# Second sine table from the first's angle, k's first block loaded ahead of x's second quarter, two ScalarE copies ahead of the fold, and the order anew

## The chip, the cores and the metric

The kernel runs on one core of a Trainium2 chip. A core has five engines with queues of their own: TensorE (PE, matrix products into PSUM; its weight loads are listed as PEld), VectorE (DVE, element-wise work), ScalarE (ACT, functions from tables, and copies), GpSimd (POOL) and SyncE (SP, which here only issues DMAs). Each engine works through its instructions in the order in which the program issues them and waits on semaphores where another engine or a transfer has to be done first. The metric is device time in microseconds (us); lower is better.

## The reference

Two parts, whose results stand side by side in the last dimension. A is dilated sliding attention over x with 32 heads of 18, a window of 8 and a dilation of 2. B is a causal long convolution with a short one ahead of it, all per channel.

```python
# S = 2048, D = 576, H = 32, Dh = 18, W = 8, dil = 2, ks = 4
def A(x, wqkv, wo):
    q, k, v = split(x @ wqkv)                       # each (H, S, Dh)
    idx = pos[:, None] - arange(W)[None, :] * dil    # 8 positions back, every second
    logits = einsum("hsd,hswd->hsw", q, k[:, idx]) * Dh ** -0.5    # idx < 0 masked
    return einsum("hsw,hswd->hsd", softmax(logits), v[:, idx]) @ wo

def B(q, k, v, shift_k, ssm_k, ssm_D):
    k_shift = sum(k shifted by t positions * shift_k[:, t] for t in range(4))
    kv = k_shift * v
    y = irfft(rfft(kv, 2 * S) * rfft(ssm_k, 2 * S))[:S]     # causal convolution over S
    return q * (y + kv * ssm_D)
```

## The kernel before, in words

All inputs are bf16. Part A is computed with the sequence along the free dimension: x is transposed (its first two quarters of 512 positions by TensorE, `transpose_x`, L477 to L481; the other two by transposing DMAs, `turn_x`), and `project` (L386) makes q, k and v tile by tile: eight matmuls of 128x512 and two for the last 64 rows, then one ScalarE copy out of PSUM (L427). `project_first` (L507) makes q's tiles for the first half of the sequence earlier. The logits are VectorE products of q with shifted k (L849) that TensorE sums over each head's rows (L864); softmax, the weighing of v (L973 with sums at L990) and the output product (L1046) follow.

Part B splits the sequence into four blocks of 512 and does the convolution as products of short spectra. For each block i, `taps(i)` (L582) is VectorE's work: k shifted and weighted by the taps `skb` and multiplied by v. `mirror(i, n)` (L610) folds the block's two halves with TensorE and copies the result back with ScalarE (L620). `x_spectrum(i)` (units "fx", L793 and L795) and `filter_spectrum(m)` (units "fk", L638, L639 and L714) are matmuls with sine tables. `fold_filter(m)` (L668) prepares the filter's block m first: for m = 0 to 2 by four ScalarE copies (L674 to L677) and three indirect DMAs of POOL's queue that gather and add rows (`gather`, L652); for m = 3 by matmuls (`by_matmuls`, L683), with the copies of L691 and L692 and then two copies out of PSUM (L694). A block's spectra are multiplied on VectorE (L1126), summed over blocks on TensorE (L1154) and turned back (`inverse`, L1186), and the result is gated with q.

**Sine tables.** Each matmul table holds sines at integer phases. `table` (L449) forms the phases with two VectorE multiplications (L451) and one bitwise and (L452), and returns a ScalarE call that takes the sine of 128x1024 phases (L453). Before the change there are two tables for the filter (`table_k(0)`, `table_k(1)`) and two for x (`table_x(0)`, `table_x(1)`), a quarter period apart, and each has its own phases. The four calls stand in the list `sines` and are issued between the first projections (L554, L557, L569).

**Loads.** Nearly all loads go through SP's queue, in program order: x's first quarter, w's first part, x's second quarter (`load_x(1)`), k's first block (`load_k(0)`, six DMAs on SP and a small one on POOL's queue, and a POOL memset of three rows that lie before the sequence), w's second part, v's first block, k's second, and so on.

**The order.** Up to the projections the order is written out by hand. From there, pieces of TensorE work with their ScalarE copy ("units") lie in one list, `units`. VectorE's work is emitted in a fixed order, and at set places `until()` (L361) takes the next number out of PLACES and pops so many units from the head of the list; `need(label)` (L368) pops until no unit with that label is left. So the number tuples at the top of the file settle how the work of TensorE and ScalarE falls between VectorE's steps. Each tile of projections is two units, of which the first has 0 and the second 1 as its third argument; the code uses this to insert nothing between them. What the tuples do:

- PLACES: the first four numbers are popped after `taps(0)` to `taps(3)`, the fifth before the logits, the next five within the first half's logits (then the second half's logits, softmax and the rest).
- AT: where the mirrors of blocks 0 to 2 and fold 3 are inserted into the list.
- EARLY: how many units of filter spectrum 3 stand before, between and after the two mirrors of block 3.
- FKS and FXS: how units of the x spectra and of v's projection are mixed with those of the filter spectra 3, 2, 1, 0.
- FOLDS: where folds 2, 1 and 0 are inserted, in this order of insertion, at most at the first unit that needs them.
- REGROUP: before which steps of the logits VectorE regroups v's weights.
- ZMIX, BY_DMA, PRE: when, in the loop over n = 1 to 26 at L1315, spectral products begin, and which sums of spectra go by DMA (`third`, L1067: an SP copy and an adding DMA of POOL's queue). A number above 26 in BY_DMA or PRE is never reached.

PSUM is two pools, tags A and B, of two buffers each: a unit's matmuls wait until an earlier unit's ScalarE copy has freed a buffer.

Of the kernel before, what the change touches and what calls it, by code (L numbers as in the profile page):

```python
# [16 lines left out]
PSUM = bass.MemoryType.PSUM  # L17

ZMIX = (
    3, 1, 0, 0, 1, 5,  # L20
)

PRE = (
    27, 33,
)

TOGETHER = (
# [3 lines left out]
THIRDS = ((0, 0), (0, 1), (1, 1)), ((0, 2), (1, 2)), ((0, 3), (1, 3))  # L31

BY_DMA = (
    37, 32, 21,
)

REGROUP = (
    0, 7,
)
# [6 lines left out]
FKS = (  # L46
    5, 1, 0, 0, 0, 0, 0, 0, 0, 0, 0, 0, 0, 0, 0, 0, 0, 0, 0, 2, 0, 0, 0, 0, 0, 1, 0, 0, 2, 0,
)
FXS = (
    0, 1, 1, 25, 2, 0, 0, 0, 0,  # L50
)

FOLDS = (
    2, 5, 9,
)

EARLY = (
    0, 0, 6,
)

AT = (
    0, 8, 9,
)


# [6 lines left out]
def kernel(  # L72
# [13 lines left out]
    nc = tc.nc  # L86
# [92 lines left out]
    nc.scalar.dma_start(skrow[96:97, :], B_shift_k.rearrange("d j -> (d j)").unsqueeze(0))  # L179
    warm = sp1.tile([128, 1], FP32, name="warm")  # L180
    nc.scalar.activation(warm[:], pib[:], ACT.Sin)
# [29 lines left out]
    def load_k(i):  # L211

        eng = nc.sync
        kj = sp1.tile([128, 7, D], BF16, name="kj", bufs=2)
        r0 = BL * i
        low = [(0, 64)]
        if i == 0:
            nc.gpsimd.memset(kj[0:1, 0:3, :], 0.0)
            nc.gpsimd.dma_start(kj[0:1, 3:7, :], kf[0:4, :].unsqueeze(0))
            low = [(1, 49), (49, 64)]  # L220
        for a, b in ((3, 7), (0, 3)) if i == 0 else ((0, 7),):
            for p0, p1 in low:
                eng.dma_start(kj[2 * p0:2 * p1:2, a:b], bass.AP(
                    tensor=kf.tensor, offset=kf.offset + (r0 + 4 * p0 - 3 + a) * D,
                    ap=[[4 * D, p1 - p0], [D, b - a], [1, D]]))
            eng.dma_start(kj[1:128:2, a:b], bass.AP(tensor=kf.tensor, offset=kf.offset + (r0 + 256 + 3 - a) * D,
                                                    ap=[[4 * D, 64], [-D, b - a], [1, D]]))
        kjs.append(kj)
# [217 lines left out]
    nc.vector.tensor_copy(rp[:], rp_i[:])  # L446
    nc.vector.tensor_scalar(rp[64:128, 4:8], rp[64:128, 4:8], -510.0, None, op0=ALU.add)

    def table(n_i, T, vec, cols, period, offs):  # L449
        for n in range(2):  # L450
            nc.vector.tensor_scalar(n_i[:, n, :], vec, rp[:, cols[n]:cols[n] + 1], offs[n], op0=ALU.mult, op1=ALU.add)  # L451
        nc.vector.tensor_single_scalar(n_i, n_i, period - 1, ALU.bitwise_and)  # L452
        return lambda: nc.scalar.activation(T, n_i, ACT.Sin, bias=pib[:], scale=-2.0 * np.pi / period)  # L453

    def table_k(c):
        return table(n_all[:, 2 * c:2 * c + 2, :], TK[:, c, :, :], n_all[:, 8, :], (2 + c, 2 + c), 2048, (256.0, 1792.0))

    def table_x(n):
        return table(n_all[:, 4 + 2 * n:6 + 2 * n, :], TX[:, 2 * n:2 * n + 2, :], n_all[:, 8, :], (4, 5), 4096,
              (512.0 + 1024.0 * n,) * 2)  # L460

    def table_i(s):

# [204 lines left out]
    def fold_filter(m):  # L668
# [14 lines left out]
        def by_matmuls():  # L683
            pss = [bank2("ps_rev", "A") for _ in range(2)]
            for c in range(2):
                turns = ((flip0, 1 - c), (corner, c), ((identn0, identn)[c], 2 + c))
                for n, (w, of) in enumerate(turns):
                    for h in range(2):
                        nc.tensor.matmul(pss[c][:, h, 0:HD], w[:], kt[:, of, HD * h:HD * h + HD], start=(n == 0),
                                         stop=(n == len(turns) - 1))  # L690
            nc.scalar.activation(other(m), kt[:, 2, :], ACT.Copy, scale=keep2[:])  # L691
            nc.scalar.activation(row(m, 2), row(m, 2), ACT.Copy, scale=0.5 / KAPPA)  # L692
            for c in range(2):
                nc.scalar.activation(halves(kt[:, c, :]), pss[c][:, :, 0:HD], ACT.Copy, scale=0.5)  # L694
                pe(0.7, "A", 0.65)
            nc.gpsimd.dma_start(view(Ks, k_at(m, 2) + 2 * D, [[1, 2 * D]]), view(Ks, k_at(m, 2), [[1, 2 * D]]),
                                accum_op=ALU.add, max_dma_last_dim=2 * D)
            nc.gpsimd.dma_start(other(m), kt[:, 0, :], accum_op=ALU.add)

        if m == NBL - 1:  # L700
            return (1.4, by_matmuls, f"fold{m}")
        return (0.0, unit, f"fold{m}")

    def filter_spectrum(m):
# [27 lines left out]
    def add_half(t, to, of):  # L732
        nc.gpsimd.dma_start(half(t, to), half(t, of), accum_op=ALU.add, max_dma_last_dim=HB)

    def turn_filter(m):
        for part in range(2):
            add_half(Ks, k_at(m, part), k_at(m - 1, part))
# [3 lines left out]
    for i in range(NBL):  # L741
# [634 lines left out]
```

## Time and profile before

| what | value |
|---|---|
| median of 3 runs | 214.44 us (214.31 to 215.56) |
| the profiled execution | 215.43 us |
| its span in the profile | 213.7 us |
| instructions | 5043 |
| matmuls on TensorE | 2094 |
| DMA traffic | 40.84 MB, 191 GB/s on average |

The page's slices show how evenly the engines are busy; each digit is the busy share of a fortieth of the span (5.3 us) in tenths:

```profile
PE   7899899999597989998999999999999999999891
...
DVE  7999999999989948969888999989969999899952
ACT  4699788765989989988358878864865887765540
POOL 8999990001958888422175000002029002313000
PEclk9999999999969999999999999999999999999998
DMA  6999999998153587999999999494779977995133
```

A 9 is 90% or more. PEclk is the clock granted to TensorE in tenths of full speed. A row of the timeline gives the start in us, the duration in us, the engine, the line of the kernel, the operation, what is written and read with its shape, how many instructions the row merges, and in brackets the idle time of the engine just before it with what ended that idle time. An engine name with a small q stands for its sequencer, where DMAs are issued; SPq is the loads' queue. The DMA table's last column is the time from issue to landing. Where a wait names an engine that had long been done, the real releaser was another one, often a DMA.

### The profile page before, as it was taken

Reading aid. Unit: us, or ns where it says so; the run is one execution under the profiler, and the core shown is the slowest. Engines: PE = TensorE matmul, PEld = TensorE weight load, DVE = VectorE, ACT = ScalarE, POOL = GpSimd, SP = SyncE. Lnnn points to the kernel's source line nnn. Section 1 sums busy time; section 2 is a strip of 40 time slices with the busy share of each in tenths; the row PEclk is TensorE's granted clock in tenths of the full one; section 3 lists DMA queues with packets and bytes.
Section 4 is the critical chain, followed back from the end, with each engine's and each line's share of the span. In section 5 each row is a group of like instructions: output and inputs, shape, how many; then the busy total and the mean of one; then the engine's idle time right before and its main releaser. Section 6 shows DMA issues by size and latency. Waiting matters only on the chain.

```text
span 213.7 us, 5043 instructions
## 1 busy us (share of the span) xinstructions
PE 199.4 (93%) x2094; PEld 109.7 (51%) x2094; DVE 191.5 (90%) x143; ACT 156.1 (73%) x226; POOL 83.6 (39%) x106
## 2 busy tenths in 40 slices
PE   7899899999597989998999999999999999999891
PEld 3443444344342455465334666666566667676660
DVE  7999999999989948969888999989969999899952
ACT  4699788765989989988358878864865887765540
POOL 8999990001958888422175000002029002313000
PEclk9999999999969999999999999999999999999998
DMA  6999999998153587999999999494779977995133
GB/s 203 294 323 235 240 326 330 217 239 227 59 83 55 86 114 104 181 188 150 220 237 238 207 217 215 72 225 140 155 276 195 205 224 254 215 236 198 38 110 110
DMA packets 35866, 40.84 MB, mean 191 GB/s; under 512 B 17442, under 2 KB 28834, under 8 KB 35844
## 3 DMA queue, kind: packets, MB, share of 16 engines
q1 hardware_dynamic: 27490, 25.76, 46.5%
q0 software_dynamic: 5888, 12.25, 31.6%
q10 hardware_dynamic: 2466, 2.51, 3.5%
q8 instruction: 16, 0.26, 0.5%
q14 instruction: 6, 0.05, 0.1%
HBM read 15.32 MB, written 5.61 MB: 98 GB/s over the span
## 4 chain that ended last, share of the span: by engine, by line
PE 34%; issue 8%; DMA 7%; DVE 4%; ACT 4%; POOL 2%; ACTq 0%; DVEq 0%; POOLq 0%
PE ps_z L1154 9%; PE ps_inv L1186 7%; PE ps_wo L1046 6%; PE ps_acc L990 6%; DMA Ks<-Ks 4%; PE ps_fx L793 3%; DMA qk<-in_A_wo_dram 3%; DVE av L973 2%; ACT av L1167 2%; PE ps_wo L1038 1%; DVE qk L973 1%; POOL qk L1022 1%; ACT qk L994 1%; DVE TB L1195 1%; PE ps_back L1227 1%
## 5 line engine op out<-in xcount | busy, mean ns | idle before, releaser
L391 PE MATMUL ps_proj<-xw 128*128 128x512 bf16 x160 | 38.1, 380 | 0.5 <-ACT qk L427 0.5
L849 DVE TENSOR_TENSOR av<-qk 128x4096 bf16<-128x4096 bf16 (+1 forms) x16 | 31.7, 2020 | 4.5 <-PE ps_log L864 3.9
L391 PEld LDWEIGHTS <-xw 128*128 128x128 bf16 x160 | 14.2, 98 | 20.2 <-issue 5.9
L1126 DVE TENSOR_TENSOR qk<-xw,Ks 128x2304 bf16<-128x2304 bf16 x16 | 21.0, 1349 | 0.0
L427 ACT ACTIVATE qk<-ps_proj 128x1024 bf16<-128x1024 f32 x14 | 14.3, 1025 | 8.7 <-PE ps_proj L402 4.1
L1167 ACT ACTIVATE av<-ps_z 128x768 bf16<-128x768 f32 x20 | 15.3, 809 | 6.7 <-PE ps_z L1154 6.7
L714 ACT ACTIVATE Ks<-ps_fk 128x576 bf16<-128x576 f32 x32 | 18.7, 666 | 1.6 <-PE ps_fk L639 1.6
L588 DVE TENSOR_TENSOR tB<-kj,skb 128x4608 bf16<-128x4608 bf16 (+1 forms) x8 | 19.3, 2418 | 0.1
L795 ACT ACTIVATE xw<-ps_fx 128x576 bf16<-128x576 f32 x32 | 18.5, 662 | 0.8 <-PE ps_fx L793 0.8
L793 PE MATMUL ps_fx<-xw,TB 128*128 128x288 bf16 x128 | 17.9, 286 | 1.1 <-ACT v L427 0.5
L652 POOL DMA_INDIRECT Ks<-bounce,from_row x8 | 16.4, 2053 | 5.1 <-ACT Ks L676 3.0
L1046 PE MATMUL ps_wo<-qk 128*128 128x288 bf16 x128 | 17.9, 287 | 0.0
L638 PE MATMUL ps_fk<-Ks,TB 128*128 128x384 bf16 x62 | 17.5, 339 | 0.1
L1073 POOL DMA_DIRECT2D xw<-xw x3 | 3.6, 1204 | 32.4 <-DMA xw<-xw 30.9
L990 PE MATMUL ps_acc<-av,ident 64*64 64x512 bf16 x160 | 15.7, 378 | 0.2 <-DVE av L973 0.2
L639 PE MATMUL ps_fk<-Ks,TB 128*128 128x192 bf16 x62 | 15.7, 253 | 0.0
L793 PEld LDWEIGHTS <-TB 128*128 128x128 bf16 x128 | 11.9, 98 | 7.2 <-issue 4.2
L973 DVE TENSOR_TENSOR av<-Ks,v 128x4096 bf16<-128x4096 bf16 x6 | 13.7, 2289 | 2.0 <-PE ps_acc L990 1.1
L1046 PEld LDWEIGHTS <-qk 128*128 128x128 bf16 x128 | 11.5, 98 | 5.9 <-issue 3.4
L1189 ACT ACTIVATE v<-ps_inv 128x576 bf16<-128x576 f32 (+1 forms) x14 | 9.5, 675 | 6.9 <-PE ps_inv L1186 6.9
L994 ACT ACTIVATE qk<-ps_acc 128x1024 bf16<-128x1024 f32 x8 | 8.2, 1024 | 8.1 <-PE ps_acc L990 8.1
L1186 PE MATMUL ps_inv<-av,TI 128*128 128x288 bf16 (+1 forms) x96 | 13.4, 293 | 0.6 <-ACT av L1167 0.6
(196 smaller groups left out, 458.0 us busy)
## 6 DMA issues: line engine op xcount, KB each, us to landing
Ks<-Ks POOLq DMA_DIRECT2D x8, 576.0 KB, 6.7
TB<-av SPq DMA_DIRECT2D x12, 256.0 KB, 6.1
kj<-in_B_k_dram SPq DMA_DIRECT2D x6, 504.0 KB, 5.7
vt<-in_B_v_dram SPq DMA_DIRECT2D x8, 288.0 KB, 5.0
Ks<-av SPq DMA_DIRECT2D x8, 256.0 KB, 6.7
xw<-xw SPq DMA_DIRECT2D x3, 576.0 KB
xw<-xw POOLq DMA_DIRECT2D x3, 576.0 KB, 8.7
Ks<-in_A_x_dram SPq DMA_DIRECT2D x2, 576.0 KB, 4.1
```

Of the source, the lines that this page charges most:

```text
L391: nc.tensor.matmul(ps[:, jp, :], wq(kb, comp, 128 * ct, 128), xT(kb, 1024 * jj + 512 * jp, 512), **se)
L588: dve(2304 * n, lambda: nc.vector.tensor_tensor(to, view(kj, row * D, [[D, n], [D, 4], [1, D]]), view(skb, row * D, [[D, n], [0, 4], [1, D ...
L714: nc.scalar.activation(view(Ks, k_at(m, cs ^ (m & 1)) + 96 * gi, [[768, 3], [384, 2], [1, 96]]), acc3(ps), ACT.Copy, scale=(PSG, MSG)[cs][ ...
L793: nc.tensor.matmul(ps[:, pm, 0:HD], TX[:, 2 * pm + c, 128 * gi:128 * gi + 128], kv[:, 2 * c + pm, HD * h:HD * h + HD], start=(c == 0), sto ...
L849: return P, at, step, dve(1024 * nj, lambda: nc.vector.tensor_tensor(view(P, at, [[step, 4], [256, nj], [1, 256]]), view(t, o + 256 * hh, ...
L973: r = dve(4096, lambda: nc.vector.tensor_tensor(view(P, 0, [[2048, 2], [256, W], [1, 256]]), X, view(v, voff + 2 + 256 * hh, [[512, 2], [2 ...
L990: nc.tensor.matmul(acc[64 * o:64 * o + 64, h, :], ident[64 * h:64 * h + 64, 64 * h:64 * h + 64], view(P, 256 * u, [[2048, 2], [1, 256]])[6 ...
L1046: nc.tensor.matmul(ps[:, r, 0:HD], oT(hh, 2 * c + r, t)[:, o:o + 128], wo[:, t // 2, t % 2, HD * h:HD * h + HD], start=(t == 0 and h == 0) ...
L1126: r = dve(3 * QTR, lambda: nc.vector.tensor_tensor(pr, view(xw, HB * XG[i] + QTR * t, [[HB, 3], [1, QTR]]), view(Ks, k_at(j - i, 0) + QTR ...
L1154: nc.tensor.matmul(view(acc[r], 512 * h, [[192, 2], [96, 2], [1, 96]])[o:o + 64], w[64 * h:64 * h + 64, 64 * h:64 * h + 64], pr[64 * h:64 ...
L1167: nc.scalar.activation(y, z, ACT.Copy)
L1186: nc.tensor.matmul(ps[:, c, 0:n], TI[:, sl, pm, 128 * c:128 * c + 128], Y(j, pm)[:, sl, c0:c0 + n], start=(pm == 0 and sl == 0), stop=(sl ...
```

## The change

Four edits and a new set of order numbers.

1. `table` now makes both tables of a pair from one set of phases: VectorE forms the phases once, ScalarE takes the sine (first table), then the absolute value of the same angle into fp32, and later the sine of a quarter turn minus or plus that absolute value (second table). Two [128, 1] constants for the quarter turns are set by POOL.
2. `load_k(0)` moves ahead of `load_x(1)`. The three rows before the sequence are filled by a DMA on ScalarE's queue from a zeroed row, in place of the POOL memset.
3. The two ScalarE copies of fold 3 that need no matmul (L691, L692) become `kept`, which is issued with the first half of the next projection tile that starts behind the list's second unit.
4. Numbers in ZMIX, PRE, BY_DMA, REGROUP, PLACES, FKS, FXS, FOLDS, EARLY and AT.

```diff
-    3, 1, 0, 0, 1, 5,
+    3, 1, 0, 0, 0, 2,
 PRE:       -27, 33,      +30, 32,
 BY_DMA:    -37, 32, 21,  +38, 30, 24,
 REGROUP:   -0, 7,        +2, 15,
 PLACES = (
-    6, 11, 13, 5, 1, 1, 3, 4, 11, 3, 9, 3, 3, 1, 2, 5, 3, 4, 0, 5, 0, 5, 5, 6, 2, 5, 4, 1, 2, 1, 2, 12, 2, 2, 3,
-    1, 0, 5, 1, 2, 0, 3, 1, 9, 12, 1, 1, 0, 2, 11, 0, 0,
+    3, 14, 13, 6, 1, 3, 3, 2, 10, 4, 11, 0, 4, 0, 3, 5, 3, 4, 1, 4, 0, 5, 5, 5, 3, 5, 4, 1, 2, 1, 2, 12, 2, 2, 3,
+    1, 0, 5, 1, 2, 4, 4, 0, 5, 6, 1, 1, 0, 11, 0, 8, 2,
 FKS (30 numbers):  second 1 -> 0, twelfth 0 -> 1
 FXS:       -0, 1, 1, 25, 2, 0, 0, 0, 0,   +0, 1, 1, 24, 0, 0, 0, 1, 0,
 FOLDS:     -2, 5, 9,     +0, 8, 5,
 EARLY:     -0, 0, 6,     +0, 1, 6,
 AT:        -0, 8, 9,     +0, 5, 15,
...
+    quarter_turn = {}
+    for sign in (-1, 1):
+        quarter_turn[sign] = sp1.tile([128, 1], FP32, name="quarter_turn", bufs=2)
+        nc.gpsimd.memset(quarter_turn[sign][:], float(np.float32(-0.5 * sign * np.pi)))
...
         if i == 0:
-            nc.gpsimd.memset(kj[0:1, 0:3, :], 0.0)
+            nc.scalar.dma_start(kj[0:1, 0:3, :], view(xw[0:1], 0, [[0, 4], [1, 432]]))
...
     load_w(nc.sync, 0)
+    load_k(0)
     load_x(1)
...
-    load_k(0)
     load_w(nc.sync, 1)
...
+    def table(at, cols, period, off, T, sign):
+        n_i = n_all[:, at:at + 2, :]
         for n in range(2):
+            nc.vector.tensor_scalar(n_i[:, n, :], n_all[:, 8, :], rp[:, cols + n:cols + n + 1], off, op0=ALU.mult,
+                                    op1=ALU.add)
         nc.vector.tensor_single_scalar(n_i, n_i, period - 1, ALU.bitwise_and)
+        mag = view(Ks, 8 * HB, [[1, 4 * HB]]).bitcast(FP32).rearrange("p (n f) -> p n f", n=9)[:, at + 2:at + 4, :]
+
+        def first():
+            nc.scalar.activation(T[0], n_i, ACT.Sin, bias=pib[:], scale=-2.0 * np.pi / period)
+            nc.scalar.activation(mag, n_i, ACT.Abs, bias=pib[:], scale=-2.0 * np.pi / period)
+
+        def second():
+            nc.scalar.activation(T[1], mag, ACT.Sin, bias=quarter_turn[sign][:], scale=float(sign))
...
-    sines = [table_k(0), table_k(1)]
+    sines = table_k()
...
-    sines += [table_x(0), table_x(1)]
+    sines += table_x()
...
-            nc.scalar.activation(other(m), kt[:, 2, :], ACT.Copy, scale=keep2[:])
-            nc.scalar.activation(row(m, 2), row(m, 2), ACT.Copy, scale=0.5 / KAPPA)
...
+        def kept():
+            nc.scalar.activation(other(m), kt[:, 2, :], ACT.Copy, scale=keep2[:])
+            nc.scalar.activation(row(m, 2), row(m, 2), ACT.Copy, scale=0.5 / KAPPA)
...
         if i == 2:
-            mirrors.append(fold_filter(3))
+            kept, fold3 = fold_filter(3)
+            mirrors.append(fold3)
+            n = next(n for n, u in enumerate(units) if n > 1 and getattr(u[1], 'args', ())[2:3] == (0,))
+            units[n] = units[n][:1] + (partial(behind, units[n][1], kept),) + units[n][2:]
```

The lines with several numbers on one line stand for tuples of the file, old after the minus and new after the plus. `behind(f, g)` calls f and then g.

More of the change, by code (lines that the diff above doesn't have):

```diff
@@ L19 @@
 ZMIX = (
[L20 removed]
+    3, 1, 0, 0, 0, 2,
 )
 PRE = (
[L24 removed]
+    30, 32,
 )
@@ L447, with table_k, table_x @@
     nc.vector.tensor_scalar(rp[64:128, 4:8], rp[64:128, 4:8], -510.0, None, op0=ALU.add)
-    def table(n_i, T, vec, cols, period, offs):
+    def table(at, cols, period, off, T, sign):
+        n_i = n_all[:, at:at + 2, :]
         for n in range(2):
-            nc.vector.tensor_scalar(n_i[:, n, :], vec, rp[:, cols[n]:cols[n] + 1], offs[n], op0=ALU.mult, op1=ALU.add)
+            nc.vector.tensor_scalar(n_i[:, n, :], n_all[:, 8, :], rp[:, cols + n:cols + n + 1], off, op0=ALU.mult,
+                                    op1=ALU.add)
         nc.vector.tensor_single_scalar(n_i, n_i, period - 1, ALU.bitwise_and)
[L453 to L460, printed above, removed]
+        mag = view(Ks, 8 * HB, [[1, 4 * HB]]).bitcast(FP32).rearrange("p (n f) -> p n f", n=9)[:, at + 2:at + 4, :]
[4 more added lines that the diff above has]
+            nc.scalar.activation(T[1], mag, ACT.Sin, bias=quarter_turn[sign][:], scale=float(sign))
+        return [first, second]
+    def table_k():
+        return table(0, 2, 2048, 256.0, [TK[:, :, n, :] for n in range(2)], -1)
+    def table_x():
+        return table(4, 4, 4096, 512.0, [TX[:, 2 * n:2 * n + 2, :] for n in range(2)], 1)
     def table_i(s):
```

19 lines of the change are left out of this document (11 added, 8 removed).

## The prediction

> **What bounds the kernel now.** I read the page's busy table and its slices first, then the busy time in windows, then TensorE's rows of the timeline for its idle time. The profiled execution took 215.43 us, 213.7 of them its span; the median of the runs shown is 214.44, so 0.99 less. The sum below is made against 215.43 and then carried to the median.
>
> ```profile
> PE 199.4 (93%) x2094; PEld 109.7 (51%) x2094; DVE 191.5 (90%) x143; ACT 156.1 (73%) x226; POOL 83.6 (39%) x106
> ...
> 5.00:10.00 5.00, 4.38 (x33) 2.24 (x34) 4.90 (x11) 3.43 (x5) 4.78 (x9) 1.00 1.09 301
> 30.00:35.00 5.00, 5.00 (x34) 1.96 (x29) 4.93 (x4) 3.48 (x5) 1.89 (x4) 1.00 1.06 388
> ...
> 55.00:60.00 5.00, 2.45 (x23) 1.29 (x21) 5.00 (x4) 4.24 (x9) 4.70 (x4) 0.90 0.21 63
> 60.00:65.00 5.00, 4.80 (x40) 2.17 (x39) 4.41 (x3) 4.69 (x8) 2.02 (x5) 0.76 0.59 89
> 65.00:70.00 5.00, 3.45 (x37) 1.47 (x39) 5.00 (x5) 5.00 (x10) 4.62 (x2) 1.00 0.41 59
> ...
> 165.00:170.00 5.00, 5.00 (x66) 3.21 (x65) 5.00 (x5) 4.33 (x7) 0.55 (x1) 1.00 1.04 185
> ```
>
> A window's row gives its length, the busy time of PE, PEld, DVE, ACT and POOL, the granted clock, the DMA share and GB/s. TensorE works without a break at 30 to 35 and at 165 to 170 us; from 55 to 70 it doesn't, and there ScalarE is at 4.24 to 5.00 of 5. So the kernel has three stages: projections that TensorE sets, a stretch from about 55 to 83 us that ScalarE sets, and a long rest that TensorE sets again. VectorE is nearly as busy, but TensorE's waits name it once, for 0.40 us:
>
> ```profile
> 24.16 1.89 PE L391 MATMUL ps_proj<-xw 128*128 128x512 bf16 x8 [0.54 <-ACT qk L427]
> 58.72 1.22 PE L617 MATMUL ps_fold<-xw,fold 128*64 128x288 bf16 x8 [2.49 <-ACT xw L620]
> 65.20 0.62 PE L864 MATMUL ps_log<-av,E 128*32 128x512 bf16 x8 [0.40 <-DVE av L849]
> 69.78 0.62 PE L864 MATMUL ps_log<-v,E 128*32 128x512 bf16 x8 [1.35 <-ACT Ks L714]
> 75.50 0.65 PE L793 MATMUL ps_fx<-xw,TB 128*128 128x288 bf16 x4 [0.54 <-ACT v L427]
> ...
> 200.46 1.46 PE L1186 MATMUL ps_inv<-av,TI 128*128 128x384 bf16 x8 [0.58 <-ACT av L1167]
> ```
>
> The first five are TensorE's waits from 11 to 82 us, 5.32 us in all. The longest, 2.49 us, also costs clock: at 0.90 and 0.76 the next two windows lose (0.10 + 0.24) x 5 = 1.7 us. So TensorE loses about 7.0 us here. After 82 us no wait is over the 0.58 of the last row, so a time that TensorE is late at 97 us, when the last filter spectrum is done, is carried to the end.
>
> The Trainium skill, "TensorE: Matmul & The Clock Gate", section "What's actually happening", puts the drop to half clock after at least one idle window of some 3.4 us. By that rule the wait of 2.49 us would cost no clock; the rows show that it did, so the measurement decides.
>
> **The tables (VectorE).** Each pair of sine tables needs one phase calculation instead of two.
>
> ```profile
> 2.53 1.53 POOL L218 MEMSET kj<- 1x1728 bf16 x1
> 2.85 1.23 DVE L446 CAST rp<-rp_i 128x8 f32<-128x8 int32 x1
> ...
> 8.07 0.93 DVE L451 TENSOR_SCALAR Ks<-Ks,rp 128x512 int32<-128x512 int32 x2
> 9.03 0.69 DVE L452 TENSOR_SCALAR Ks<-Ks 128x1024 int32<-128x1024 int32 x1
> ...
> 11.65 1.39 DVE L588 TENSOR_TENSOR xw<-kj,skb 128x2304 bf16<-128x2304 bf16 x1 [0.34 <-ACT qk L517]
> ```
>
> Two of four such groups go: 2 x (0.93 + 0.69) = 3.2 us. The cast of 128x8 ran beside the memset of one row; with that memset gone (a ScalarE-queue DMA takes its place) I take 0 to 1.1 us more. VectorE could thus start the taps at about 8.9 instead of 11.65, if k is there. This is worth nothing at the end while TensorE sets the pace; its cover is TensorE's projections up to 55 us.
>
> **k ahead of x's second quarter (SP's queue).** Six DMAs of k pass one of x.
>
> ```profile
> Ks<-in_A_x_dram SPq DMA_DIRECT2D x1, 576.0 KB, 4.1
> ...
> 3.13 0.59 SPq L207 DMA_DIRECT2D Ks<-in_A_x_dram  x1
> 3.77 1.56 SPq L223 DMA_DIRECT2D kj<-in_B_k_dram  x2
> ...
> 7.78 0.66 SPq L226 DMA_DIRECT2D kj<-in_B_k_dram  x1
> 8.49 0.60 SPq L167 DMA_DIRECT2D xw<-in_A_wqkv_dram  x1
> ...
> kj<-in_B_k_dram SPq DMA_DIRECT2D x1, 216.0 KB, 5.1
> ...
> 10.34 1.07 PE L480 MATMUL ps_x<-ident,Ks 128*128 128x128 bf16 x16
> ...
> 3.63 0.38 ACT L529 ACTIVATE skb<-ps_sk 128x256 bf16<-128x256 f32 x1 [0.72 <-PE ps_sk L526]
> ```
>
> The first row is x's first quarter on an empty queue: 4.1 us from issue to landing. The 216 KB row is k's last piece, issued at 7.78, landed at 12.9. At 5 to 10 us the DMA share is 1.09, so this queue is full. Moved, k's six start 0.64 us earlier and x's quarter starts at 3.13 + (8.49 - 3.77) = 7.85. The bytes up to its end are those that lay ahead of 12.9 before: it lands at about 12.9; at best, with 4.1 us, at 11.95. TensorE reaches its transposes (L480) at 10.34 to 10.41 and has nothing else in its order: it stands for 2.5 us, from 1.5 to 2.5. Behind L480 stand all projections. k's own last piece comes near 11, so the taps start about 2 us earlier. Nothing else on SP's queue moves: w's second part still issues at 8.49. The new DMA on ScalarE's queue issues before that engine's copy at 3.63, where it idles 0.72: nothing. On POOL's queue load_k's DMA keeps its place, two tiny memsets come and one of 1.53 us goes: nothing.
>
> **Two Abs (ScalarE).** The trace has no Abs; the nearest row is the sine of the same shape.
>
> ```profile
> 15.29 1.14 ACT L453 ACTIVATE TB<-Ks,pib 128x1024 bf16<-128x1024 int32 x1
> 16.52 1.02 ACT L517 ACTIVATE qk<-ps_proj 128x1024 bf16<-128x1024 f32 x1
> ...
> 18.89 1.02 ACT L517 ACTIVATE qk<-ps_proj 128x1024 bf16<-128x1024 f32 x1 [0.31 <-PE ps_proj L515]
> ...
> 26.30 0.68 PE L617 MATMUL ps_fold<-xw,fold 128*64 128x288 bf16 x8
> ...
> 1.41 1.28 ACT L181 ACT_TABLE_LOAD   x1 [1.41 <-PEq L1360]
> ```
>
> I take 1.14 each, bounds 1.02 (a copy of that size) and 1.14 + 2 x 1.28 (if Abs switched tables; copies stand between sines in these rows with no load). Two Abs add 2.1 us of ScalarE, back to back; ScalarE's own small waits between 15 and 24 us, 0.31 the longest, some 0.9 in all, take a part up; the rest, 1.2, comes at TensorE's wait of 24.16, ahead of which a mirror of 0.68 now stands as cover. I count +0.5. So TensorE ends the projections 2.5 + 0.5 = 3.0 us later.
>
> The Trainium skill, "ScalarE: Activation LUTs", section "Table sets: the hidden batching unit", says that abs is in every table set, which gives no load; no run here shows an Abs yet.
>
> **The two copies (L691, L692).**
>
> ```profile
> 53.59 1.02 ACT L427 ACTIVATE qk<-ps_proj 128x1024 bf16<-128x1024 f32 x1 [1.03 <-PE ps_proj L395]
> ...
> 55.58 0.79 ACT L691 ACTIVATE Ks<-Ks,keep 128x576 bf16<-128x576 bf16 x1
> 56.39 0.68 ACT L692 ACTIVATE Ks<-Ks 1x576 bf16<-1x576 bf16 x1
> ...
> 59.92 1.19 ACT L620 ACTIVATE xw<-ps_fold 128x576 bf16<-128x576 f32 x2 [0.72 <-PE ps_fold L617]
> ...
> 62.01 0.65 ACT L714 ACTIVATE Ks<-ps_fk 128x576 bf16<-128x576 f32 x1 [0.31 <-PE ps_fk L639]
> ```
>
> They now stand behind k's last tile's first half, where ScalarE waits 1.03 us; they take 1.37, so 1.03 of it is hidden and 0.34 delays one copy. TensorE's wait of 2.49 us shrinks to about 0.6, and ScalarE's own waits of 0.72 and 0.31, which the slow clock made, go. From 53.6 us the chain runs through ScalarE: 3.0 - 1.03 - 1.03 = +0.9 us at 83 us. By then the new order has done two filter units more and one x unit less, 0.4 us of TensorE, so +0.5 net.
>
> **The order anew (FOLDS, PLACES; POOL's queue).** Worked out from the lists, FOLDS (0, 8, 5) emits fold 2, fold 0, fold 1 instead of 2, 1, 0. Each puts three gathers (L652) on POOL's queue.
>
> ```profile
> 64.83 1.82 POOL L652 DMA_INDIRECT Ks<-bounce,from_row  x1 [2.98 <-ACT Ks L676]
> ...
> 79.25 1.94 POOL L652 DMA_INDIRECT Ks<-bounce,from_row  x1 [0.30 <-ACT Ks L714]
> ...
> 82.61 0.33 PE L638 MATMUL ps_fk<-Ks,TB 128*128 128x384 bf16 x1
> ...
> Ks<-bounce,from_row POOLq DMA_INDIRECT x8, 5.3
> ```
>
> The first and the seventh gather are 14.42 us apart, 2.4 each. TensorE starts filter spectrum 1 at 82.61; its gather was the fourth (64.83 + 3 x 2.4 + 5.3 = 77.3, 5 us in hand). Now it is the seventh: 79.25 + 5.3 = 84.6, plus 0.3 as ScalarE reaches fold 2 that much later. Spectrum 2 is finished ahead, so TensorE arrives at about 82.8: it stands 1.9 us, bounds 0 (POOL starts sooner) and 2.5. ScalarE's first softmax exponent waits behind these units, and with it VectorE's next step. Spectrum 0, last in the order, gains time that nothing waits for. ZMIX, BY_DMA's third number (24 for 21: one SP copy and one POOL add three steps later) and the later PLACES only permute work where TensorE is never idle: 0, bounds -0.5 and +0.5. BY_DMA's first two numbers and PRE lie beyond the loop's 26 steps or as before: nothing.
>
> **Sum.** +0.5 at 83 us, +1.9 at spectrum 1, 0 later: +2.4 us. 215.43 + 2.4 = 217.8 for an execution like the profiled one, 214.44 + 2.4 = 216.8 at the median. Low end of the bounds: 1.5 for x and 0 for the gathers give -0.5 - 0.5 (tail) = 213.4; high end: 2.5 for the gathers and +0.5 in the tail, 217.9.
>
> **Rivals.** (1) Same: the gathers are not late, as POOL's chain starts sooner or TensorE arrives later; then +0.5, 214.9. For it: POOL stood idle 2.98 us before 64.83. Against: it waited there for fold 2's copies, which come no earlier. (2) Faster: x's late quarter is swallowed. TensorE's loss of 7.0 us between 11 and 82 is replaced by x's 2.5, 1.0 at the wait of 24.16 and 0.8 around the last mirror, 4.3, and the new order leaves no other wait up to 97: -2.7, 211.7. It decides if the waits left between 61 and 97 us stay under 2.7. For it: VectorE is 2 us ahead and ScalarE has 1.03 + 1.03 less to wait for. Against: that stretch is ScalarE's, which has the same copies to make. (3) The new 2.5 us stand at 10.4 drops the clock, as 2.49 us did at 58.7: +1.7, 218.5. For it: the drop followed a wait of just this length. Against: the trace has only that one case. (4) Abs switches tables: four loads of 1.28 on ScalarE ahead of the waiting tiles, +4 or so, 220.8.
>
> **How the numbers follow.** Forecast 0.48, its own range 215.8 to 217.9; same 0.26; faster 0.20; clock 0.05; tables 0.01. I call within 1% (212.3 to 216.6) no change, about what a measurement of this kernel can tell. Some 0.11 of the forecast's chance lies below 216.6, so: slower 0.37 + 0.06 = 0.43, same 0.26 + 0.11 = 0.37, faster 0.20. The range 212.0 to 218.1 leaves out half of the faster case, the clock and the tables.
>
> **What would show it.** x: TensorE's first L480 of the second quarter near 12.9 instead of 10.34, after a wait on a DMA of x. Tables: two L451 pairs fewer, taps from about 9.6. Abs: rows near 1.14, no third table load. Copies: they lie before the last L427 copy of k, no wait of 2 us at the last L617, clock 1.00 from 55 to 65. Order: L652's seventh to ninth land after TensorE has reached spectrum 1, a wait there named for a DMA. I am wrong if x's transposes start by 11, if that wait is absent, or if TensorE's waits from 61 to 97 sum to under 2.7 us.

## The result, and the profile after

The changed kernel takes 222.36 us (median of 4 runs, 221.44 to 223.1) against 215.0 for the kernel before (4 runs): 1.0359 times as long, interval 1.0304 to 1.0413. The profiled execution took 222.42 us, 220.7 of them its span; before it was 215.43 and 213.7. Ratios here and below leave disturbed executions out; medians are over all of them.

Line numbers have moved: x's transposes are now L494 (before L480), the filter spectra L652 and L653 (L638, L639), the gathers L666 (L652), VectorE's products of the logits L872 (L849).

Of the page after, the span, two engines and the slices of the clock:

```profile
span 220.7 us, 5030 instructions
...
PE 200.3 (91%) x2085; PEld 112.0 (51%) x2094; DVE 188.1 (85%) x137; ACT 157.2 (71%) x228; POOL 78.0 (35%) x107
...
PEclk9969999999999999699999999999999999999997
```

TensorE is busy for about as long (200.3 us, 199.4 before), so most of the 7 us is standing time, and some is slow clock. Its longest waits from 5 to 105 us, and the end of the last filter spectrum, from the timeline after:

```profile
13.09 1.80 PE L494 MATMUL ps_x<-ident,Ks 128*128 128x128 bf16 x16 [2.74 <-DMA Ks<-in_A_x_dram]
...
29.41 1.89 PE L395 MATMUL ps_proj<-xw 128*128 128x512 bf16 x7 [0.99 <-ACT qk L431]
...
67.28 0.32 PE L652 MATMUL ps_fk<-Ks,TB 128*128 128x384 bf16 x1 [1.41 <-ACT Ks L730]
...
88.94 0.50 PE L652 MATMUL ps_fk<-Ks,TB 128*128 128x384 bf16 x1 [5.08 <-DMA Ks<-bounce,from_row]
...
104.27 0.24 PE L653 MATMUL ps_fk<-Ks,TB 128*128 128x192 bf16 x1
```

The 1.41 at 67.28 is about matched by a wait of 1.35 that the kernel before has at 69.78. The last row ends at 104.5. In the kernel before the same row is:

```profile
97.41 0.25 PE L639 MATMUL ps_fk<-Ks,TB 128*128 128x192 bf16 x1
```

It ends at 97.66. What follows is as long as it was: 220.7 - 104.5 = 116.2 us against 213.7 - 97.7 = 116.0. So the whole loss lies ahead of the last filter spectrum, and the windows up to there give its parts. After:

```profile
5.00:50.00 45.00, 40.89 (x258) 18.43 (x262) 41.72 (x29) 33.96 (x43) 18.68 (x38) 0.96 1.04 281
50.00:104.52 54.52, 46.22 (x396) 24.25 (x397) 39.06 (x27) 43.70 (x70) 33.48 (x21) 0.97 0.63 108
...
9.82:13.23 3.41, 0.67 (x5) 0.18 (x6) 3.24 (x3) 1.02 (x1) 3.22 (x5) 1.00 1.00 326
13.23:16.64 3.41, 3.19 (x22) 2.22 (x22) 3.34 (x3) 1.14 (x2) 3.30 (x3) 0.50 1.09 381
...
84.91:88.32 3.41, 0.00 (x0) 0.00 (x0) 3.22 (x6) 0.02 (x1) 2.80 (x3) 1.00 0.68 95
88.32:91.73 3.41, 2.79 (x12) 1.80 (x13) 3.41 (x2) 1.30 (x2) 3.41 (x3) 0.50 0.92 134
```

And before:

```profile
5.00:50.00 45.00, 43.84 (x292) 18.73 (x294) 43.94 (x35) 34.75 (x44) 25.69 (x40) 1.00 1.08 272
50.00:97.66 47.66, 42.29 (x374) 22.25 (x371) 41.30 (x28) 42.28 (x68) 32.02 (x21) 0.96 0.69 118
...
55.58:58.99 3.41, 0.92 (x13) 0.68 (x13) 3.41 (x3) 3.38 (x7) 3.10 (x3) 1.00 0.29 92
58.99:62.40 3.41, 3.35 (x24) 1.45 (x23) 3.27 (x2) 2.38 (x5) 2.87 (x5) 0.50 0.39 59
```

The first number behind the length is TensorE's busy time. It stood idle for (45.00 - 40.89) + (54.52 - 46.22) = 12.41 us after and 1.16 + 5.37 = 6.53 before: 5.9 more. Half clock costs half of the busy time in its windows: (3.19 + 2.79) / 2 = 3.0 us after, 3.35 / 2 = 1.7 before: 1.3 more. Together 7.2, a little more than the 104.5 - 97.7 = 6.9 by which the end comes later. Two places hold most of it: the wait for x at 13.09 and the wait for a gather at 88.94, each followed by half clock.

### The profile page after: what moved, and what is told of

The parts are those of the page before. It is cut to its first block, busy times and chain, and to the rows that moved or that the text cites. A ratio compares the mean times of both kernels' runs of the same rounds, so it can differ in the third digit from the quotient of the medians.

```text
span 220.7 us, 5030 instructions
## 1 busy us (share of the span) xinstructions
PE 200.3 (91%) x2085; PEld 112.0 (51%) x2094; DVE 188.1 (85%) x137; ACT 157.2 (71%) x228; POOL 78.0 (35%) x107
## 4 chain that ended last, share of the span: by engine, by line
PE 65%; ACT 19%; DMA 8%; issue 4%; DVE 1%; SPq 1%; ACTq 0%; DVEq 0%
PE ps_proj L395 14%; PE ps_z L1177 8%; PE ps_inv L1209 7%; PE ps_acc L1013 7%; PE ps_wo L1069 6%; PE ps_fx L816 6%; DMA Ks<-bounce,from_row 3%; PE ps_fk L652 3%; ACT Ks L730 3%; DMA xw<-in_A_wqkv_dram 3%; PE ps_log L887 2%; PE ps_proj L406 2%; DMA Ks<-in_A_x_dram 2%; ACT av L1190 1%; ACT qk L431 1%
## 5 line engine op out<-in xcount | busy, mean ns | idle before, releaser
L872 DVE TENSOR_TENSOR av<-qk 128x4096 bf16<-128x4096 bf16 (+1 forms) x16 | 31.9, 2025 | 13.7 <-PE ps_log L887 8.9
L395 PE MATMUL ps_proj<-xw 128*128 128x512 bf16 x152 | 37.0, 380 | 1.6 <-ACT qk L431 1.0
L652 PE MATMUL ps_fk<-Ks,TB 128*128 128x384 bf16 x62 | 17.6, 338 | 7.5 <-DMA Ks<-bounce,from_row 5.1
L666 POOL DMA_INDIRECT Ks<-bounce,from_row x8 | 19.0, 2372 | 4.2 <-ACT Ks L690 2.1
L816 PE MATMUL ps_fx<-xw,TB 128*128 128x288 bf16 x128 | 18.5, 291 | 0.6 <-ACT xw L818 0.4
L653 PE MATMUL ps_fk<-Ks,TB 128*128 128x192 bf16 x62 | 15.7, 253 | 0.0
L431 ACT ACTIVATE v<-ps_proj 128x1024 bf16<-128x1024 f32 x9 | 9.1, 1016 | 6.0 <-PE ps_proj L395 4.5
```

The costliest lines, as they stand in the source:

```text
L395: nc.tensor.matmul(ps[:, jp, :], wq(kb, comp, 128 * ct, 128), xT(kb, 1024 * jj + 512 * jp, 512), **se)
L431: nc.scalar.activation(view(t, o + pad + 1024 * jj, [[512, 2], [1, 512]]), ps[:], ACT.Copy)
L652: nc.tensor.matmul(o[:, 0:2], w, rhs[:, 0:2], start=start, stop=stop)
L666: nc.gpsimd.indirect_dma_start(to, None, rows, bass.IndirectOffsetOnAxis(ap=from_row[:, n:n + 1], axis=0), compute_op=ALU.add)
L816: nc.tensor.matmul(ps[:, pm, 0:HD], TX[:, 2 * pm + c, 128 * gi:128 * gi + 128], kv[:, 2 * c + pm, HD * h:HD * h + HD], start=(c == 0), sto ...
L872: return P, at, step, dve(1024 * nj, lambda: nc.vector.tensor_tensor(view(P, at, [[step, 4], [256, nj], [1, 256]]), view(t, o + 256 * hh, ...
```

## The experiments

**Which of the two orders costs what.** Four runs. The first puts x's second quarter ahead again, the second the folds, the third both; the fourth makes only the load order's change in the kernel before.

```diff
e1:  the changed kernel, and
-    load_k(0)
     load_x(1)
+    load_k(0)
e2:  the changed kernel, and FOLDS   -0, 8, 5,   +0, 5, 8,
e3:  the changed kernel, and both
e4:  the kernel before, and
+    load_k(0)
     load_x(1)
...
-    load_k(0)
```

> The changed kernel with x's second quarter issued ahead of k's first block again; the rest as changed. Theory (the late quarter costs its wait and the clock behind it, and both are carried to the end): the wait of 2.74 us at L494 goes, and with it the stretch at half clock from 13.2 to 16.6 us, some 1.7 us of work: 222.4 - 4.4 = 218.0 us, granted clock near 1.00 from 10 to 20 us, and the wait at the first filter spectrum (5.08 us) stays within 1 us. Rival (the stretch from 55 to 83 us, which ScalarE and POOL set, swallows the gain, because the gathers start no earlier): TensorE is earlier there and waits longer at L652, 7 us or more, and the time stays at 221 to 222.

Measured: 215.2 us, 0.9994 of before (0.9949 to 1.0039). By this ratio the late quarter is worth all of the loss, far more than the 4.4 us expected; neither theory gave that. The ratio is less sure than its interval: these four executions lie at 213.9 to 218.76 us, the longest, which was profiled, still waits 4.66 us at spectrum 1, and four more of the same kernel, further down, lie at 215.77 to 225.32. The median of all eight is 216.8 us.

> The changed kernel with FOLDS (0, 5, 8), so that fold 1 is issued ahead of fold 0 and its gathers are the fourth to sixth on POOL's queue instead of the seventh to ninth; the rest as changed. Theory (the order of the folds makes the wait at spectrum 1): no wait on a DMA over 0.5 us at L652, no half clock from 88 to 92 us: 222.4 - 5.1 - 1.7 = 215.6 us, at worst 217 if the moved unit costs something. Rival (POOL's chain of gathers is late in any order): a wait of 2.5 us or more comes back at another filter spectrum, and the time is 218.5 or more.

Measured: 218.72 us, 1.0181 (1.0144 to 1.0218). The gather wait is gone, as the theory said, but the time is the rival's. The waits that come in its place are not at a filter spectrum, where the rival put them. From its timeline:

```profile
70.21 0.61 PE L887 MATMUL ps_log<-v,E 128*32 128x512 bf16 x8 [1.30 <-ACT Ks L730]
74.71 0.41 PE L412 MATMUL ps_proj<-xw 64*64 64x512 bf16 x4 [2.04 <-DVE xw L941]
```

> The changed kernel with both put back: x's second quarter ahead of k's first block, and fold 1 ahead of fold 0; tables, the two copies and the other order numbers as changed. Theory (the two orders hold the whole loss, and tables and copies gain): 222.4 - 4.4 - 6.8 = 211.2, taken to be 211 to 213, faster than the kernel before (215.0 us) by 2 us or more. Rival (the two Abs and the other order numbers cost what the copies gain): 214.5 to 216, no different from before.

Measured: 216.41 us, 1.0064 (1.0027 to 1.0100): the rival's side. With x in time, these runs show no gain from the old fold order (e1 is at 0.9994, with the spread just told); with x late it saves 1.0359 - 1.0181, about 1.8%. So the late quarter costs most where the fold order is new.

> The kernel before with one edit: k's first block is issued ahead of x's second quarter. Theory: TensorE waits 2.3 to 2.8 us for x near 10.4 us, half clock follows for some 3.4 us (1.7 us of work), and the delay of 4.2 us is carried on to the end: 215.0 + 4.2 = 219.2 us; VectorE, without the tables' change, is early by no more than 0.5 us. Rival (the stretch that ScalarE sets from 55 to 83 us swallows a part): the wait of 2.49 us at the last fold matmul shrinks, and the time is 215 to 217.5.

Measured: 217.07 us, 1.0125 (1.0071 to 1.0178). Its profile has the wait (2.39 us at 12.79), no half clock behind it, and the old wait at the last mirror as long as ever:

```profile
12.79 1.07 PE L480 MATMUL ps_x<-ident,Ks 128*128 128x128 bf16 x16 [2.39 <-DMA Ks<-in_A_x_dram]
...
61.16 0.97 PE L617 MATMUL ps_fold<-xw,fold 128*64 128x288 bf16 x8 [2.49 <-ACT xw L620]
```

So alone the late quarter costs about its wait: the medians are 217.07 - 214.78 = 2.3 us apart, not 7.

**The other parts alone, in the kernel before.** Tables and copies (e8), the fold order (e5), all ten tuples of numbers (e10); and in the changed kernel TensorE kept at work through the wait for x (e9).

```diff
e8:  the changed table(), table_k(), table_x(), quarter_turn, kept() and behind()
e5:  FOLDS   -2, 5, 9,   +2, 8, 5,
e10: ZMIX to AT as in the change
e9:  the changed kernel, and ahead of the transposes of x's second quarter
+    ps = bank2("ps_warm", "A")
+    for _ in range(12):
+        nc.tensor.matmul(ps[:, 0, :], ident[:], xT(0, 0, 512), start=True, stop=True)
```

> The kernel before with the new sine tables and the two copies moved ahead of fold 3; loads and all order numbers as before. Theory (these two edits gain): the wait of 2.49 us at the last mirror falls under 1 us, no half clock from 55 to 65 us, the two Abs add up to 1 us near 24 us: 215.0 - 1.7 - 1.7 + 0.5 = 212.1 us, taken to be 211.5 to 213.5. Rival (the stretch that ScalarE and POOL set from 55 to 83 us takes the gain back as other waits at L638 or L864): 214 to 215.5, no difference.

Measured: 215.41 us, 0.9990 (0.9961 to 1.0019): the rival. The wait at the last mirror is shorter and the clock stays up, but the time comes back in other waits, among them these on VectorE, one past 105 us:

```profile
58.02 0.97 PE L631 MATMUL ps_fold<-xw,fold 128*64 128x288 bf16 x8 [1.15 <-ACT xw L634]
...
64.64 0.61 PE L887 MATMUL ps_log<-av,E 128*32 128x512 bf16 x8 [1.59 <-DVE av L872]
...
119.33 0.40 PE L1013 MATMUL ps_acc<-qk,ident 64*64 64x512 bf16 x2 [1.25 <-DVE qk L996]
```

> The kernel before with one edit: FOLDS (2, 8, 5), so that fold 0 is issued ahead of fold 1. Theory (the gather of spectrum 1 is then the seventh): TensorE waits 2 to 5 us at L638 for a gather near 82 us, half clock may follow: 217 to 221 us. Rival (with the other old numbers TensorE comes later or POOL's chain starts sooner): no wait over 1 us there, 214.5 to 216.

Measured: 216.58 us, 1.0097 (1.0066 to 1.0128). TensorE waits for three gathers, 1.46 + 0.41 + 0.67 = 2.5 us in all. So with the other old numbers the new fold order costs something even where x is in time.

> The kernel before with the ten changed tuples of order numbers and nothing else: x's second quarter first, old tables, the two copies inside fold 3. The run with x first, tables, copies and the new numbers took 215.2 us. Theory (tables and copies gain some 2.5 us, the numbers cost as much): 217 to 219 us, with a wait of 4 to 5 us at the gather of spectrum 1. Rival (the numbers are made for the changed code and gain or cost nothing alone): 214.5 to 216.

Measured: 216.14 us, 1.0077 (1.0038 to 1.0116), between the two theories, with a wait of 2.46 us for the gather.

> The changed kernel with 12 matmuls of 128x512 whose result nothing reads, issued by TensorE ahead of the transposes of x's second quarter, so that it works through the wait of 2.74 us there. Theory (half clock follows from TensorE's standing still, and its work is carried to the end): no half clock from 13 to 17 us, 222.4 - 1.7 = 220.7 us. Rival 1 (the clock falls whatever TensorE does there): 222 to 223. Rival 2 (the stretch that ScalarE and POOL set takes it back): full clock at 13 to 17 us, but 222.

Measured: 221.47 us, 1.0317 (1.0276 to 1.0358). In the profiled execution the granted clock is 1.00 from 10 to 20 us, as it should be if half clock follows from TensorE's standing still; one execution alone doesn't show it. The gain of 0.4% lies within the intervals of this run and of the changed kernel; its size isn't settled.

**Why the two orders multiply.** Load order and numbers together, without tables and copies:

```diff
e14: the kernel before, with e4's load order and e10's numbers
```

> The kernel before with k's first block ahead of x's second quarter and the ten tuples of order numbers; tables as before and the two copies inside fold 3. Alone the load order cost 2.2 us and the numbers 1.2. Theory (the late quarter and the new order of folds make more of each other: every us of delay goes through ScalarE to POOL's chain of nine gathers): 219 us or more, with a wait of 3 us or more at spectrum 1. Rival (they add up, and tables or copies make the rest of the loss): 217.5 to 218.5.

Measured: 222.18 us, 1.0358 (1.0335 to 1.0381), the same as the whole change (1.0359). Alone the two cost 1.25% and 0.77%; together 3.6%. So 1.5%, over 3 us, is made by their meeting, and tables and copies add nothing that these runs can tell. Of the six executions of e14 the profiled one, 220.45 us, is one of two short ones; the other four lie at 222.17 to 222.37. Where the extra loss arises is seen on POOL. The first, second and seventh gather of e10, and then of e14, from their timelines:

```profile
62.46 1.69 POOL L652 DMA_INDIRECT Ks<-bounce,from_row  x1 [0.76 <-ACT Ks L676]
64.45 1.83 POOL L652 DMA_INDIRECT Ks<-bounce,from_row  x1 [0.30 <-ACT Ks L714]
...
77.10 1.83 POOL L652 DMA_INDIRECT Ks<-bounce,from_row  x1 [0.31 <-ACT Ks L714]
```

```profile
64.81 2.94 POOL L652 DMA_INDIRECT Ks<-bounce,from_row  x1 [2.12 <-ACT Ks L676]
68.05 3.14 POOL L652 DMA_INDIRECT Ks<-bounce,from_row  x1 [0.31 <-ACT xw L674]
...
80.52 3.03 POOL L652 DMA_INDIRECT Ks<-bounce,from_row  x1 [0.30 <-ACT Ks L714]
...
86.87 0.50 PE L638 MATMUL ps_fk<-Ks,TB 128*128 128x384 bf16 x1 [4.60 <-DMA Ks<-bounce,from_row]
```

The first gather waits for ScalarE's copy of fold 2 and starts 2.35 us later, about as much as x was late (2.41). But the seventh ends at 83.55 instead of 78.93, 4.6 later: three of the seven take 3 us in place of 1.7 to 1.8, and only the third, the fourth and the sixth are shorter, by 0.6, 0.6 and 0.4. TensorE itself is only 2.4 us later there, so it waits 4.60 us instead of 2.46. Why a gather takes longer shows beside VectorE. POOL and VectorE of the changed kernel, with its first, second and seventh gather (start, duration):

```profile
66.41 2.94 POOL L666 DMA_INDIRECT Ks<-bounce,from_row  x1 [2.12 <-ACT Ks L690]
...
69.06 2.29 DVE L872 TENSOR_TENSOR v<-qk 128x4096 bf16<-128x4096 bf16 x1
...
69.65 3.14 POOL L666 DMA_INDIRECT Ks<-bounce,from_row  x1 [0.30 <-ACT xw L688]
...
80.22 3.50 DVE L872 TENSOR_TENSOR av<-qk 128x2048 bf16<-128x2048 bf16 x2 [1.69 <-PE ps_log L887]
...
82.12 3.03 POOL L666 DMA_INDIRECT Ks<-bounce,from_row  x1 [0.30 <-ACT Ks L730]
```

The second gather ends at 72.79, 1.44 us after the product that was running (69.06 + 2.29 = 71.35); the seventh at 85.15, 1.43 us after 83.72. So it looks as if a gather waits for VectorE's running instruction. Two runs halve these products: e12 in the changed kernel, e13 with x first (e1):

```diff
-            return P, at, step, dve(1024 * nj, lambda: nc.vector.tensor_tensor(
...
+            def parts():
+                for u in range(0, 4, 2) if hh == 0 else (0,):
+                    nu = 2 if hh == 0 else 4
+                    nc.vector.tensor_tensor(
+                        view(P, at + u * step, [[step, nu], [256, nj], [1, 256]]),
...
+            return P, at, step, dve(1024 * nj, parts)
```

> The changed kernel with VectorE's products of the first half of the heads (L872) made in two instructions of half the size each. In every trace so far a gather that POOL issues while VectorE works ends 1.42 to 1.52 us after a VectorE instruction ends, and takes 1.55 us while it idles. Theory (a gather waits for the VectorE instruction that is running): the longest remainder halves, so gathers take at most 1.45 + 1.2 = 2.65 us instead of 3.14, the first and the seventh gather are 13 to 14.5 us apart instead of 15.7, the wait at spectrum 1 falls from 5.08 to 3 to 4 us: 219.5 to 221.5 us. Rival (the gathers are slow by themselves or by other transfers): durations of 3 us and a wait of 5 us stay, 222 to 223.5.

Measured: 218.63 us, 1.0202 (1.0169 to 1.0235): 3.7 us less than the changed kernel, by an edit that only adds VectorE instructions. First and seventh gather are 13.91 us apart, none takes over 2.56 us, and the wait at spectrum 1 falls from 5.08 to 1.95 with no half clock behind it, more than expected:

```profile
66.26 1.66 POOL L666 DMA_INDIRECT Ks<-bounce,from_row  x1 [2.12 <-ACT Ks L690]
...
80.17 2.02 POOL L666 DMA_INDIRECT Ks<-bounce,from_row  x1 [0.30 <-ACT Ks L730]
...
85.67 0.34 PE L652 MATMUL ps_fk<-Ks,TB 128*128 128x384 bf16 x1 [1.95 <-DMA Ks<-bounce,from_row]
```

The Trainium skill, "SBUF — State Buffer", section "Who interferes with whom", says that a VectorE instruction with two SBUF inputs contends with a GpSimd instruction that reads SBUF, over a port pair that one of them holds for its whole instruction. The rows above agree: the products have two SBUF inputs, and the wait is for the product's end. The same section tells of a probe in which `tensor_tensor`, the kind of these products, did not stall a DMA, and infers a reason. These gathers are DMAs that POOL issues, and they wait, so here the measurement decides.

> Both: x's second quarter first, and VectorE's products halved. Theory: no gather over 2.65 us, the wait at spectrum 1 under 1.5 us: 213 to 214.5 us, faster than the kernel before by up to 1 us. Rival (VectorE's added instructions cost what the gathers gain): 215 to 216.

Measured: 226.32 us, 1.0552 (1.0528 to 1.0576); both theories miss. Its first two gathers and VectorE beside them:

```profile
63.02 3.55 DVE L875 TENSOR_TENSOR av<-qk 128x2048 bf16<-128x2048 bf16 x4
66.50 2.35 DVE L875 TENSOR_TENSOR v<-qk 128x2048 bf16<-128x2048 bf16 x2
...
61.68 8.68 POOL L666 DMA_INDIRECT Ks<-bounce,from_row  x1 [2.12 <-ACT Ks L690]
...
70.67 7.02 POOL L666 DMA_INDIRECT Ks<-bounce,from_row  x1 [0.30 <-ACT Ks L689]
```

From 55.1 to 76.2 us VectorE has no gap between its instructions, and the gather issued at 61.68 isn't let in before 68.85. TensorE then waits 4.06, 1.63 and 3.58 us for gathers, and its clock stays at half from 79.49 to 96.56. The missing gap alone doesn't explain it: in e12 VectorE has none from 65.18 to 78.4 us either, and the five gathers there take 1.66 to 2.56 us. Why they get in there and not here stays open. The kernel with x first and whole products was run again:

> The same kernel as the run with x's second quarter first; in the profile of that run one gather took 5.59 us, twice any other, and half clock lasted 6.83 us. Theory (x's lateness costs 7 us because it is added to twice: 4.8 us at the first filter spectrum, and some 2.6 more by a later and slower chain of gathers): a first gather near 61.6 us of 3 us or less, the wait at spectrum 1 at 1 to 2.5 us, the last spectrum's end near 97.5 us against 104.5 in the changed kernel, and 214 to 215.5 us. Rival (the gathers' wait of 4.66 us is there without the disturbance too, and the 7 us come from behind it): a wait over 4 us, and a tail behind the last spectrum that is shorter than 116 us.

Measured: 215.77 to 225.32 us in four executions, too scattered for a ratio. In the profiled one, of 217.8 us, the first gather takes 5.62 us and the wait at spectrum 1 is 2.71 us; the tail behind the last spectrum is 216.1 - 99.9 = 116.2 us. So the rival's place is wrong, and the theory's calm first gather isn't there either: the first gather gets in late in this kernel too. Four runs then put a tiny VectorE instruction ahead of each product of the first half of the heads: e15 in e13, e16 in e1, e17 in the changed kernel, e18 in e8.

```diff
+    pause = main.tile([128, 8], I32, name="pause")
+    nc.vector.memset(pause[:], 0)
...
+                    if hh == 0:
+                        nc.vector.tensor_single_scalar(pause[:], pause[:], 0, ALU.bitwise_or)
```

> The kernel with x first and halved products (226.3 us) with a VectorE instruction of 128x8 int32, whose result nothing reads, ahead of each halved product. Theory (gathers starve while VectorE's products follow one another without a gap, and get in at an instruction of another kind): no gather over 2.7 us, the first and the seventh 15 us apart or less, 213 to 215.5 us. Rival 1 (only a gap lets a gather in, and the small instruction leaves none): gathers of 7 to 9 us stay, 226. Rival 2 (the halved products make VectorE the bound): no long gather, but 218 or more.

Measured: 213.61 us, 0.9985 (0.9949 to 1.0020): 12.7 us less than e13. No gather ahead of the ninth takes over 2.12 us, and TensorE no longer waits for one:

```profile
61.60 1.89 POOL L668 DMA_INDIRECT Ks<-bounce,from_row  x1 [2.12 <-ACT Ks L692]
...
74.17 2.11 POOL L668 DMA_INDIRECT Ks<-bounce,from_row  x1 [0.30 <-issue]
```

> The kernel with x first (213.9 to 218.8 and more, its first gather 5.6 us in both profiles) with the same small instruction ahead of each whole product of the first half of the heads. Theory: the first gather takes 3.2 us or less, the wait at spectrum 1 is 0 to 1.5 us, and the time is steadier, 213 to 214.5 us. Rival (no change of the gathers): 215 to 219.

Measured: 219.82 us, 1.0213 (1.0173 to 1.0252). The first gather still takes 5.77 us, past two of the small instructions, and gets in at 66.3 where VectorE pauses; so they alone don't let a gather in, though with halved products the long gathers went away with them. What decides at which end a gather gets in, the runs don't tell.

> The changed kernel with the same small instructions. In its trace no gather waited for more than the product that was running. Theory: the gathers keep their 1.55 to 3.1 us, the wait at spectrum 1 stays 4 to 5.5 us, 222 to 223 us. Rival (the small instructions speed or slow VectorE's own chain so that the gathers meet other products): 219 to 221.5 or over 223.

Measured: 222.28 us, 1.0369 (1.0331 to 1.0407), as the theory said; the wait is 4.56 us.

> The kernel before with the new tables, the two copies ahead of fold 3, and the small instructions. Without these it ran at 213.9 to 216.2 us, no different from before. Theory (its gathers aren't late, so nothing is gained): 214 to 215, no difference. Rival (steadier gathers take the wait of 1.25 us at 119 us and the spread away): 213 to 213.8.

Measured: 214.58 to 221.62 us, too scattered for a ratio; inconclusive.

**Is anything left to gain.** e15 once more, and e19, its edit of the products (halves and small instructions) in the kernel before:

> The same kernel as the run with x first, halved products and pauses. Theory (the two waits held the whole loss, tables and copies gain a little): 213.3 to 214.0 us, 0.3 to 0.6% under the kernel before. Rival (no difference): ratio 0.998 to 1.002.

Measured: 215.67 us, 0.9999 (0.9962 to 1.0036): no difference. The executions of this kernel lie at 213.3 to 213.7 or at 215.3 to 216.3. The profile of an upper one has a first gather of 2.59 us in place of 1.89 and a wait of 1.64 us at spectrum 1 that the lower one lacks.

> The kernel before with its products of the first half of the heads halved and the small instructions ahead of them, nothing else. Theory (its gathers have 5 us in hand at spectrum 1, so they gain nothing; VectorE isn't the bound): 214.3 to 215.3 us, no difference. Rival (the chain of gathers sets the kernel before too): 213 to 213.8.

Measured: 215.13 us, 1.0013 (0.9975 to 1.0050): no difference, as the theory said. No version here beats the kernel before by more than the intervals allow.

## Why the prediction was right or wrong

Slower was right; 216.8 us and the range up to 218.1 were too low by 5.6 and 4.3.

- **x's second quarter: right.** Landing forecast for 12.9, stand 2.5 us; measured 13.09 and 2.74. Its issue moved to 8.55 (forecast 7.85).
- **Half clock behind it: wrong.** It was rival (3), priced right (1.7 us; measured 3.19 / 2 = 1.6) and given 0.05, although the one row of before that showed a wait of this length showed the drop. The runs show that such a wait can go either way: 2.74 us dropped the clock, and so did 2.38 in e12, but 2.39 in e4 didn't. So no single price was right; that it came here was the execution's phase (last section).
- **Two Abs: right.** They take 1.14 and 1.15 us, no table load follows, and the wait at k's second tile is 0.99, 0.45 more than before (forecast 0.5). The Trainium skill, "ScalarE: Activation LUTs", section "Table sets: the hidden batching unit", had abs in every table set; the trace agrees.
- **Tables on VectorE: right.** The taps start at 9.96 (forecast 9.6) and e8 shows no gain from it.
- **The two copies: right in their place, nothing at the end.** The wait at the last mirror and its half clock are gone, as forecast. e8 shows that tables and copies come to 0.9990 (0.9961 to 1.0019): other waits take their place.
- **The order anew: the failed step.** The prediction put the seventh gather at "79.25 + 5.3 = 84.6, plus 0.3", and the stand at 1.9 us with 2.5 as its upper bound. That holds for the new order alone: 2.5 us in e5, 2.46 in e10. In the changed kernel the chain of gathers starts at 66.41, where the prediction had 64.83 + 0.3, since ScalarE's copies are late with x (it starts at 64.81 in e14, whose profiled execution has no half clock at 13 us, and at 62.46 in e10, with x in time); it needs 15.71 us to the seventh instead of 14.42; that gather takes 3.03 us instead of 1.94; and it lands 3.8 us after its end, where 5.3 - 1.94 = 3.4 was taken. It lands at 88.94, about 4 us (1.3 + 1.3 + 1.1 + 0.4) after the forecast 84.9, and the wait is 5.08. The working took the pace of the gathers, 2.4 us each, from a trace with x in time and kept it; e12 shows that VectorE's instructions set it.
- **The tail: right.** 116.2 us behind the last spectrum, 116.0 before.
- **The sum.** Forecast was a start of spectrum 1 that is 0.5 + 1.9 = 2.4 us late (from its own 84.9 and 82.8 the stand is 2.1, not 1.9). TensorE reached it at 88.94 - 5.08 = 83.86, 1.25 later than the 82.61 of before, and started at 88.94: 6.3 late. In this 1.25 is all that came ahead, among it the 1.6 us of half clock at 13 us and the 1.7 no longer lost at 59 us. Behind the wait the sum had no term for half clock: 2.79 / 2 = 1.4 us. Of 6.3 + 1.4 = 7.7, about 0.9 comes back, because less work and waiting is left up to the last spectrum; 6.9 was measured there.
- **The rivals.** "Same" and "faster" needed gathers in time, or waits under 2.7 us from 61 to 97 us; the gather alone is 5.08. The fault lay in letting only 0.3 us of x's lateness through to the gathers, and in leaving their durations as they were.

## What to carry to other kernels

Before pricing a late transfer, follow its delay through every engine to the next chain with little in hand: here 2.4 us at the start met a chain of gathers whose slack an order number had just used up, and became 7. A duration on POOL that varies from row to row may belong to another engine; look at what VectorE runs at the row's start and end before taking its mean. And measure a change of load order and a change of emission order both alone and together: each looked harmless alone (1.25% and 0.77%), and together they cost 3.6%.

## What the runs showed of the hardware

**A gather issued on POOL waits for VectorE.** In the 20 traces at hand (before, after and 18 runs) there are 180 such gathers, the nine of folds 2, 1 and 0 in each: 31 take 1.54 to 1.60 us, the other 149 end 1.41 to 1.53 us after the end of a VectorE instruction, in 142 cases of the first to end after the gather's start. In e1, e13 and e16 a gather missed up to seven such ends and took up to 8.68 us. The Trainium skill's page "SBUF — State Buffer", in the section already named, lets whichever issues first hold the ports for its whole instruction; that a waiting gather can be passed over by several instructions in a row is beyond it.

**Half clock comes by a fixed grid, not by the length of a wait.** Stretches at half clock are 3.41 us or a multiple, and begin on a grid of 3.41 us whose phase differs between executions. Of the windows of this grid that ran at full clock in the 20 traces, all with TensorE idle for 1.91 us or more were followed by half clock, none with 1.77 or less. Windows of e4 show both, the second pair on the same grid:

```profile
8.15:11.56 3.41, 2.25 (x10) 0.69 (x8) 3.34 (x7) 1.76 (x2) 3.21 (x8) 1.00 1.06 294
11.56:14.97 3.41, 2.13 (x23) 1.55 (x25) 3.38 (x3) 0.74 (x1) 3.27 (x4) 1.00 1.08 326
...
59.35:62.76 3.41, 1.50 (x14) 0.88 (x14) 2.40 (x2) 2.92 (x7) 1.88 (x4) 1.00 0.01 1
62.76:66.17 3.41, 3.41 (x24) 1.21 (x23) 1.56 (x1) 3.41 (x7) 0.62 (x3) 0.50 0.85 130
```

The wait for x (10.40 to 12.79) is cut in two by the grid: its two windows stand idle for 1.16 and 1.28 us, and it costs no clock. The window at the last mirror stands idle for 1.91 us, and half clock follows. So by these numbers a wait between 1.9 and about 3.5 us (twice 1.77; an estimate) may or may not drop the clock, by the execution's phase. The Trainium skill, "TensorE: Matmul & The Clock Gate", section "What's actually happening", has the window free-running with the same length, which agrees; its "idle window" need not be wholly idle, 56% was enough here.
